# Attention and gated MLP on one core: GpSimd's pieces no longer wait for VectorE's pieces, with a new order of all pieces

## The chip, the cores and the metric

One core of a Trainium2 chip runs the whole kernel in one launch. The metric is the device time of one execution in microseconds (us); lower is better. Engines are named as in the profile: PE (TensorE, with PEld for its weight loads), DVE (VectorE), ACT (ScalarE), POOL (GpSimd), SP (SyncE, which issues nearly all DMAs).

## What is computed

Causal attention with a decay, in 8 batches of 8 heads, 576 positions, head size 64; then an MLP over the 512 joined columns, whose gate is a causal convolution of five taps.

```python
scores = scale * np.matmul(q, k.transpose(0, 1, 3, 2))
cum = np.cumsum(np.log(np.clip(f, 0.0001, 1.0)), axis=-1)
decay = cum[:, :, :, None] - cum[:, :, None, :]
scores = np.where(causal, -1000000000.0, scores + decay)
scores = scores - np.max(scores, axis=-1, keepdims=True)
attn = np.exp(scores)
x = np.matmul(attn / (np.sum(attn, axis=-1, keepdims=True) + 1e-09), v)
...
for k in range(5):
    gate_pre += conv_w[k][None, None, :] * xp[:, k:k + S, :]
out = ((1.0 / (1.0 + np.exp(-gate_pre))) * (x @ w_val)) @ w_out
```

## The kernel before

The 64 heads are worked on as 32 pairs (two heads on 128 partitions); four pairs are one batch. For each pair *i* the stages are:

- **S**: PE forms the scores of three groups of key blocks (L233 is the helper that records every matmul; `banks<-Xr` for q times k, `banks<-st,pk` for the decay). DVE adds the mask and takes the maximum (L423, `negm`), ACT takes the exponential and the row sums (L427, `P`, `zs`).
- **turn**: DVE transposes P in blocks of 32 (L462, `T`). Two copies of T into `U` (L248, class `UC`) run on ACT, POOL or DVE, and four DMAs bring the other quarters (`U<-T`), after the copies into the same tile.
- **reciprocal**: POOL or DVE adds a small number to the nine row sums (L435, `zr`), then DVE forms the reciprocal and transposes it (L439 `zr`, L440 `zt`, two instructions of 9 and 32 columns); DMAs spread `zt` over the partitions (`zd<-zt`, `zb<-zd`).
- **PV**: PE multiplies (`banks<-U,vt`); DVE reads the result out times `zb` into `x` (L519, three instructions).
- **split and gate**: for matmuls of higher precision `x` is split into `xh` (a cast, L248) and `xl` (L528, x minus xh, on POOL or DVE). The gate is a sum of five taps: either a product (L253 on ACT, L255 on POOL or DVE) and a POOL addition (L564, `gate<-gate,tm`), or one DVE instruction (L562). ACT takes the tanh (L569).
- **MLP** of a batch: PE forms the value (`Mv`: `banks<-xh,wall` and `banks<-xl,wall`, in halves of six matmuls for each 128x288 tile, the second half of which uses pairs 2 and 3 of the batch), DVE multiplies with the gate (L595, `h`), which is split into `hh` (a cast) and `hl` (L609, POOL or DVE), PE forms the output (`Mo`: `banks<-wall,hh`, `banks<-wall,hl`), ACT or DVE reads it out (L636, L638), SP stores it.

The decays of pairs 0 to 20 are made at the start (L325 to L345, `st`); those of pairs 21 to 31 in the middle, from `lnf`, which is read back by a DMA (`tm<-lnf`) and then scanned on DVE (L337). The two weights are decoded in the first 80 us (L695 to L711, ACT, DVE and POOL).

The kernel doesn't choose the order of its pieces when it is built: `ORDER` is a compressed table that was planned beforehand. It gives the sequence of all 2354 pieces, the engine of each piece that has a choice, and the PSUM bank of each tile. Each engine does its pieces strictly in that sequence, and the tile framework adds the waits that data need. On top of these the kernel adds one kind of wait by hand: while it goes through the table it remembers the last DVE piece whose class is in `PORT`, and the first instruction of every POOL piece is made to wait for it:

```python
        if e == "POOL" and turn is not None:
            tc.add_manual_dep(done[0], turn.name, wait, reason="shared port")
        elif e == "DVE" and cls in PORT:
            turn = done[-1]
```

`PORT` holds the classes of the weight decode, of the split, of the gate, of the U copies, and `rec`, which is both the nine-column addition (L435) and the reciprocal with its transpose (L439, L440).

Of the kernel before, what the change touches and what calls it, by code (L numbers as in the profile page):

```python
# [41 lines left out]
NS = (21, 11)
ORDER = (
    "c-lQuTTB$`wyvtKzTd0w)%WWAy}SB;@2<Y14~RYp@-QGL5##~UohW*e0o{o(JP5-{1bG;clL&GWKp%v0Cj-Mt6gi0^I}vmeL3bkPB*J(SK~8d{?U{%A>tAbq>s#wv>xV"
    "%EWCD+XUw{X|3t$R(3V^@>Z~_zn?}0af9<T#ba1@XOUVsi_;C*Nkw15OK1fU=eMnD3r0!u&*PzPKBYr$1=J@p}Zk*tAF!i``9&<u8g-CzsQ4s-xrKo4*poQ2jPGyEg?9"
    "sB@ZfHt8aa0IvwK8Bj8I2?vwkO{a0Zh_~(9(V;Ff*0Uva2?!)CxPcsCtQNh!E5kicndyBp;2n!O>!SR0^7)c06&s<;R$$`+)lwLT@;*5P`1bysbAn$Dh%1_db$D@!WUR"
    "9vVt5Vx3Zpr^WX-!N48MD0PjH(Sx**{yD3}H9}rFnQ%V$s(nz^PX{JDwF6td>KSf6ArhcZ@Ll)=>n4<Snv*e@X6XZcEM%x9SP!L)TWr4av{Q_EObZCaULV;*i^jnnMl<"
    "&x+R2-V6%4m<NblMs<3~f^D$;;$+G6HQ;+vpic2I-(<^k3*PP7~=B<ss!hrGwl;#%a6MPN<U{rJbdvX^WHz`ZRr#0`nfQw&@-8b$SoI3OWw;(L3oI^qb@n@(0RW$|p)Y"
    "t&YCS8lpEqBlLY}g|$TQfm)yi)-(DJ{SKK#nxmhf9i_$SS7-;626`WK3-U6292y&AZ?Y~>>uJ5TVcIoX6K$UkP+RDaS<~b-7K?P9g-{VT&Sp?i>L{z9wZ%FI?XkR6kZ~"
    "DeGQQ`?*jj3YF~Nb@2V6bF&QLH0XjfPv>NsnVHN&z|!|XJbPx6o~>}t*r<ez8}5=t6{F0<35IgXYz&mq`HNOhbU+8k|&GeK+NWEnz+kKV*M!MMgc%BW`)sYf}>{1Us1-"  # L50
    "NQM~zQFEfH*n@@=QzixHqsKUhV+zkhOy0A=j?M%k)G4~I3t{CP6ua$v%>+o&7^M9U8sxE&gfutGcsH$?>8F8v+y=)d$e{^KWUIO$hbuMkx}F^xHxZ#)5yEYGc!}nFz+3"
    "smHm+9W`1M<%-bXxcYzmSj`C)BS4qFq9`nX|yR-??ERRkvGHZCvyjtEp(gtasL}TtVYM5QTdN#tW;<ob^`9fY3JIfhhABZQ}B)WipiPz2JbN`bu&EO%g`Blg^f1kfiS|"
    "Uv_>|CE{iao|2W<MkCkYvmSc8ts9|H6F4{GNH8N$_^~OYDAL1krO(a8cxE#vJ=Q#EPu&T96(DMCKW1n0J_I<QSqwzK~v$o-ocK9^{{lT4o=z&VXPa*Dh*fUf{ms*K<FK"
    "JCG^nMG*rT71be~$VIM<zQJR{I%Ws6pLv?uFKXrXaJxiJ+>~U4@r*skTw#uj2ATcbPrMn?OWr#s!tdgCiv~q&%-hUa5zK!mJ>Y%dDfo-hqUe$68p`5ru=m(Q$Q$Nu<UR"
    "X2@&~&{^pW|Jy&`InY>Mh6jUp1KR#YWf5UnFLmYKE6?~v?@#*sZ{vxvtU<Zg-9M4gg7(K$(jM9+s=%SeoG=Px1;5g)%@<YuusJV{iHaAd47ixA(Cr1-bFRtYMRagIqm5"
    "}IsC@)o&|d_W-agk(;lmFPHC{CnJAxxMHo<N(pLvZABnI(`j*S~4PGiX)O2Qkq~>I?nx>J1;rMZ{Tl9Ps;e>CCRR|M}o_qaL@9KtUYO$tXmeA{geAlg2`aPzqsq%ZEiQ"
    "egO3PM0VcT0|B-)}Z{dUmJ6wzGwcsZ~HA^90mfqsu=4S-=_*Q{k>=Wz7%gSMOlQ<@-7oQNXNj^wcm2V}F1lI*e1cVG1K+<+uqpVqm$leJU(p^C<>yqq-;Hh9pur7dPcL"
    "Xy6q4bkPCfgH~WIv%3=rO@Gnq?hGTE!Z9n;4eZrBBg*S(W^ld=8DsYh<&620@2-8@0;k(RH*({6w}Q+ec3c&I<k}nB{xqY55M?A?Orrpj~2yyeJ$Ivm^>>6H71kNe9&5"
    "2{po3GEhzvnuTYCkZ=iY7yc^X2~i;~tQOV@&!|RZw`6?zthhtiC%z^AQGQj}ud0(vRpa8YFeAJt{#6{34yx+4A7l?@2eP*^RNgFqr)*bMNeO9<^t$lAY#5!CJrUm#-Vp"
    "98yHqu*AvvVNRhVi@xTow^T~g6iwW?L=q6|?rX)ox`O2aBbH7B&F28FfK)ABWON%dSjr5;r+spr(s)Qze!`6pSg{EB=`xG29ScWVH20G(H#lfG2F5ucV`mLlkDH3QvOq"  # L60
    "nd5?xN2H;LH<zHs#{huG<?mfN~_sX-_b@iC`uDO6223zXlJy4mo5qyv^`QB{SWDoG>T@>r^1KwSISM*2i2l#Ql8d~NI^}Vrb@G^T^Cw4$23~BK~syat3L{PqPN2P@)pg"
    "O_M&!AxTgK2daE2$AE;RBEwM~=S9%0Jj-E!lv}e)tXt%as`$)bn-;}S&r=^41$J)<YSpCX)Ni(a3MHjRPhG7<LR4c=->xMP`y4xBXI;fk_@YE#510956>QUW&&8o3ivn"
    "4;T`9nUgqhnv>Oa)&dSDeLY`T@<Py2*M?v#HzFTGfbt*xagJ)GTXubw$OBZb64*m>yN*`b+3z-Iner#dnH3iZhC8#f+jIYgg1Mt}7lXEPAcNrtmA)bZPYsMHqXk*wdBN"
    "tD1UDrteVT>WCt(7*d4wGrEt)eIsaMm|kewOnQ;VbX<K_eM-$YL3%>}P%~z}f*r-u*cBa3IgI)2P1se%32atT(yuE{t1s(+Rh(D%VjZSUO_k}GDPr2yY-=v7kLi0%b*3"
    "Sc)ih!fXf?{$3Z4>Gnw9SqxYA?lGo4ZHD!TNo`c`YN{u&lhqNc0rs9LA(G&Pv^6c5Y`=6ZcbNm8awbnTwzu{mV<343FbYyDcA_MLgc)M6UI#`I14Vf_Vtx4OncSSGMJt"
    "kzPpteDr#n5EHzSZ1(YGh~rjo?)BjW{bu0)_BELRNhfen(v#h>DrWZOSN)Jxoyg6BibtMZ`daGJGP7c9|q|r^`A@wdWKG*BWdTcOUi4?J@d3_(X?thFnurz&9zFv_Py0"
    "=>#+`5r}Vg`-EvGjYwEM=bxZnL<%o64x^CUD&gmEQRvoTm*ihSDi^uj%{{*{id1bQOhb>LYWmB((WzKrSx=xGM2AgHN>&okfHbc?iHtgx=tb}gcx?`=<Em>zQFZFNqHM"
    "%-ogN|>zVW>9L8Ez;;2EuUB@VkCjPd5xIpIIlYU51El-r8W0nsM`x0W%lvHFm3+WDpoe3^K!6!$o_oJ#4;f&>1dRFSs6B1}rhpBYVHS%id_;w6EA_?7Q|+`<UgGrP)q1"
    "P8l8<w(LCPp8ca?&E9UynD?zu4G#>T4deDf`>eg&ZZVW>JohiIcKf<v!2mfRBWmohZ5XshmUr0_vq#(u_HEa`%j#aWj45ARb}ec5k_&Y2xaf`>t_jz=>xemHJ8eF0K4p"
    "$N&YEq;_l6<Y-_3tB6OIwrv}@6_ZP~YY+@STD%WbSSHrW=HSFG1;^|p|))z<48uyvSa)*kbi?S$=`tJem5v-Xq5KJ!VBz`EfQIBZtJh`Q%oTK7?h-tofI=&5qIdxmXyY"  # L70
    "!Ke;x$bE&Uh>d!jd#<dvtD)gxEbzI&zx<+#<Yg5TONhO?x=M~yfZeh^|<?pHDf()Z8iEFt&RcrQRBF$&FBlQ*>*jTZF`=6&x~im^Vl=%8T8yRUNqh`)>=o52;SwfdaJ!"
    "2Z`!-!`N`Yj?eVrbmb`P`4(~bdj&0S~<T&BD;2w5&8kc?bj%VIFuNLoeJh#2E9l_t*NcJx_roG2egEzT5z4P7%uhd`TN9+^cX|LSg;plUWJFd7}-LcT5yVp48mg8042k"
    "r&;8UKpA%irg%$M3tB-2ZT#@T_}pI|RNV$6MbOyxZUJZ}(sF4|%t|gZ__>DWlt2bbfZwoFQkm6LPM(?>QD6xSw!_{itulYsZgzeE2~)i(kN-@JVBxlkj8y-yBaI&mEhN"
    "lAq^%U|cZ1^F0mK`Yrw#{yqNQ{f8TMj{3j2cYW(2$iE#r@V4T5pTY}z_I&%HejN5?eQ-qRW%=H?nI5`-C!}?5gnICoew!2V58>6JmQbVrp8xw07~XPd?Y;3&UY~E%|G{"
    "tfEk|R%#pqn9E_5!`;G7R>Jq@9WP)}$mG!i=NeB_*RUU#-RpE@5n7o6+P4d-3|4d+E?F*1!$hx$TAA1knI><E4G9}RUmhn!uJn#fY9G4jeM@W?$jk2LbozwBT2!+}O$o"
    "v+6CKR6!AhDMw>Bkhq{{8zj-vWDMvX2S2Cqme~FBfJp7A}jbzBpmtZycB8nbw_xv&(5l_B{Ca%kH5ho7ZG_J8Nr();}NOrb(9xlxlV)+{H(|yIOf`pGNOX8FFX+E1*|b"
    "Nwjb?}$in(?EZpbo^zB4FF);RB%<a01uSC#5RqR--C)N=|qFBHhSc`Z9mwo4bKlpC@w6QyZTfTd~yS|@&d$`Bb5<3^`jP=DfBBemc^)yiJvWHv4rvjNkefS{K6kbgo51"
    "bC14V({L4nzWxSUNTpNW10&^S+a=7lF+HBX%b~6CaAz#V&?t<1gaogx#fxeu%tE2_yRGFabv|gg-_4!(HJ9*Si3cfD+@e&G_@!nP5-2CNUC|CGLi66T9)f_(B{{5Q)ce"
    "dSWXcPJ9g92&~8U11s^XfqUWZz<-BJiJ!xR;oIR`iMHVL@Xf%-6qXnb?58y8NV+j$P1mIv>8f-p3I^u`%pjOH2YJDVu~_s;V2o(W`l9w|U6h}$4oZVH(b2@KXjSxl6bm"
    "kePX^t=j$kC%7<?K2_h?&sDBTsk9}8vP5zDc+u~t`Wb}arWwi@-Mn-dM`W9f}>Ita%<#1>-*v2^-<_(<?v;!47vpG*wLdlLhRx2dBpT6`qk8Ei@Sq@m0%u}2V@jx?6R;"  # L80
    "%NLva4_1J?o2mkkjxLksbEcJB8|j<h`vc%G7V8Qy`7e2ZU#q!^h|B0IrAVmAH0@08!crX5G%wQ0pz0bAEV>Zd+FQJd(j2rF=5TMXFR!dd@8%1-6W31E%6Vj`w3ruG4V9"
    "<DZQL{m{?D2Cm6Yd^m33z2#Lwy_t~G*N8&K?G`N{Sb4%HwES}lU?u50uk?eh9HGMa;lbFdYrypisr5Dqu;u~3h?p*w1up{G*&t+c(H-fX#e~a%Yda^C?%kk>ujpTgxO7"
    "?T`Wb$URFZ(Rpn4HLhAuu_bEao5O*-0r;lfRnT$)3;2le_uhOeD9GN0Pc^M{YlBC3-WH#BydJGnT2%zsjs;vUy8#FTa-WjN`<`JVx~ANArz&Z;}<dlibX2<!ACl?pp3c"
    "@ItmZKc0^#OT?KZk*vzi=8qHalDyPZQkrT@HW20%FZ49&PJK*DLobpY$+={E{uEK4JCR#R4(3bA&g2hCsPH;-j%dm~Nrs88e0M%lSje9xE)yAIKS>lelURyg_&d>>i{%"
    "G$i<zT^-drTLo7v9nXQ1qz+*s~Lijh@j`2}qVOtls5h2fmOpeXnXCkpk2)<RRk9wJgm7R&Y!bGe1wOwN&IrrgD1ajMvsYAeLEc(y9Fl<Oldrikpna;5C?Y*(SD&{3$(u"
    "H^a(|C@W6>q-q3wsZSAa-NZ=6{k|yiw}yt;>DsUKUzSG|5ZTq|0v89779y+>SCx!6rUG97H$+j7wU@Ie08d!*qi#TaJKlU_#pMPcrpbQHw#+@ZP8j>FAf!NrW#YNsrgh"
    "_aiO?T94$^1w~HT(ywc~QyCf}zO4X&2)MRQo1(jH(bg8X$vV@iFrN+|HQfujAsk78uf&mBs0RSKaq^~FR^@ITmKn1?}$>qqQeHi)n9irhf{?L2)0bdd13g$2ZmTlmxhf"
    ">b?#tW92;jb3>H9{)iDPJv8ndOibsNla<CzTn<m5jrB<iF75az43y1Iv}+O65ZzQ0|agMo`Kapu$Qi>p8@eD+(!PcA(4$mbngXQaSINHn<!C%E)gS;9vZQvBOSDWkrWw"
    "fR#$*ik3fhQY&|IMJe>xw8`aqK)Fk>oJ%d&`cpSl{!_|51LX>oiege3{VnU;4xzFiD09N)`9Xi}g;Hjtl$DbztcNj51x+d6DdjG|%?GT!338<mxH5B~q6(;JqL!xvmv>"
    "C9%m%9b$rTk~ISy2`ft7txDvF@L{6M)+xUz9lWy+)q-=A*{s(692VyIjR{Oe8r`ELFnvP;#~"  # L90
)
# [702 lines left out]
```

## Time and profile before

| what | value |
|---|---|
| device time, median of 3 runs | 459.16 us (458.07 to 460.58) |
| device time of the profiled execution | 463.08 us |
| its span, first to last instruction | 461.0 us |
| PE busy | 423.9 us, 92% of the span |
| DVE busy | 382.9 us, 83% |
| ACT busy | 332.3 us, 72% |
| POOL busy | 309.4 us, 67% |

The span is what the trace covers; 2.08 us of the profiled execution lie around it. The profiled execution is 0.85% longer than the median of the runs. Rows of the trace give start and length in us from the start of the span; a number in square brackets is how long the engine sat idle before that row, and the name behind `<-` is what ended that wait.

### The profile page before, as it was taken

The numbers are of one execution on the slowest core, as the hardware profiler recorded it, in microseconds if no ns is written. First come the engines' busy times: TensorE is split into PE (matmuls) and PEld (weight loads), VectorE is DVE, ScalarE is ACT, GpSimd is POOL, SyncE is SP. The second block draws the span as 40 slices with busy tenths as digits, with TensorE's granted clock in tenths as the row PEclk, the third lists the DMA queues.
The fourth block names the chain that finished last, engine by engine and source line by source line (L and its number), as shares of the span: only waits on it lengthen the run. The fifth ranks groups of instructions, "written<-read, shape, count | busy, mean of one in ns | idle before, by whom it ended". The sixth has DMA issues, their size and how long they took to land.

```text
span 461.0 us, 16758 instructions
## 1 busy us (share of the span) xinstructions
PE 423.9 (92%) x6640; PEld 359.9 (78%) x6640; DVE 382.9 (83%) x1034; ACT 332.3 (72%) x836; POOL 309.4 (67%) x310
## 2 busy tenths in 40 slices
...
GB/s 287 283 129 249 213 190 241 198 118 261 186 248 163 209 171 197 274 232 206 211 199 100 136 239 215 219 181 204 132 246 192 188 206 173 223 118 129 23 70 114
DMA packets 74847, 87.23 MB, mean 189 GB/s; under 512 B 48145, under 2 KB 48145, under 8 KB 74769
## 3 DMA queue, kind: packets, MB, share of 16 engines
...
q8 instruction: 52, 0.85, 0.9%
q10 hardware_dynamic: 144, 0.29, 0.2%
q14 instruction: 27, 0.21, 0.2%
...
## 4 chain that ended last, share of the span: by engine, by line
PE 47%; POOL 13%; DVE 13%; DMA 12%; issue 6%; SPq 5%; ACT 3%; POOLq 0%; DVEq 0%; ACTq 0%
PE banks L233 47%; POOL gate L564 6%; SPq L260 5%; DMA zb<-zd 4%; DVE banks L423 4%; DVE T L462 3%; DMA U<-T 2%; DMA vt<-in_v_dram 2%; POOL xl L528 2%; POOL U L248 2%; ACT P L427 2%; DMA sh<-in_w_val_dram 1%; POOL tm L255 1%; DMA zd<-zt 1%; DMA tm<-lnf 1%
## 5 line engine op out<-in xcount | busy, mean ns | idle before, releaser
L427 ACT ACTIVATE P<-banks,negm 128x384 f32<-128x384 f32 (+8 forms) x288 | 149.6, 528 | 46.4 <-DVE negm L423 36.4
L564 POOL TENSOR_TENSOR gate<-gate,tm 128x576 f32<-128x576 f32 x82 | 117.5, 1434 | 42.6 <-DVE tm L255 14.7
L423 DVE CUSTOM_DVE_ANT_0 banks<-banks,mk 128x512 f32<-128x512 f32 (+8 forms) x288 | 135.1, 504 | 9.6 <-PE banks L233 6.7
L462 DVE STREAM_TRANSPOSE T<-P 128x1088 f32<-128x1088 f32 (+2 forms) x96 | 110.9, 1166 | 6.6 <-DMA U<-T 3.5
L233 PE MATMUL banks<-xh,wall 128*128 128x288 f32 x512 | 108.8, 298 | 1.7 <-ACT P L427 0.9
L233 PE MATMUL banks<-Xr 64*64 64x288 f32 (+8 forms) x1280 | 103.2, 410 | 2.5 <-DMA Xr<-in_x_dram 2.5
L233 PEld LDWEIGHTS banks<-U,vt 64*64 64x64 f32 x3456 | 92.3, 136 | 14.1 <-issue 10.1
L233 PE MATMUL banks<-U,vt 64*64 64x128 f32 (+1 forms) x3456 | 93.2, 257 | 9.6 <-ACT sh L695 4.0
L233 PE MATMUL banks<-wall,hh 128*128 128x512 f32 x288 | 91.6, 399 | 0.0
L233 PEld LDWEIGHTS banks<-xh,wall 128*128 128x128 f32 x512 | 84.3, 189 | 6.0 <-ACT P L427 1.6
L233 PE MATMUL banks<-xl,wall 128*128 128x288 f32 x256 | 76.0, 297 | 4.1 <-POOL xl L528 3.9
L233 PEld LDWEIGHTS banks<-Xr 64*64 64x64 f32 x1280 | 65.0, 134 | 15.8 <-issue 5.1
L233 PEld LDWEIGHTS banks<-wall,hh 128*128 128x128 f32 x288 | 52.3, 189 | 13.2 <-DVE negm L423 1.3
L233 PE MATMUL banks<-st,pk 64*64 64x288 bf16 (+8 forms) x640 | 48.6, 297 | 11.3 <-ACT P L427 6.5
L233 PE MATMUL banks<-wall,hl 128*128 128x512 f32 x144 | 56.9, 395 | 2.3 <-POOL hl L609 2.3
L427 ACT ACTIVATION_READ_ACCUMULATOR P<-banks,negm 128x1 f32 x288 | 58.4, 203 | 0.0
L248 ACT COPY U<-T 128x1440 f32<-128x1440 f32 x37 | 51.3, 1396 | 5.9 <-PE banks L233 5.2
L233 PEld LDWEIGHTS banks<-xl,wall 128*128 128x128 f32 x256 | 48.4, 189 | 5.4 <-POOL xl L528 4.1
L233 PEld LDWEIGHTS <-pk 64*64 64x64 bf16 x640 | 26.5, 107 | 29.6 <-issue 24.9
L609 POOL TENSOR_TENSOR hl<-h,hh 128x576 fp32r<-128x576 f32 (+2 forms) x39 | 40.9, 1068 | 11.5 <-DVE gate L562 4.4
L528 POOL TENSOR_TENSOR xl<-x,xh 128x576 fp32r<-128x576 f32 x24 | 34.7, 1446 | 15.9 <-DVE zt L440 10.4
L519 DVE TENSOR_TENSOR x<-banks,zb 128x256 f32<-128x256 f32 (+1 forms) x96 | 30.8, 345 | 11.5 <-PE banks L233 5.5
(103 smaller groups left out, 495.8 us busy)
## 6 DMA issues: line engine op xcount, KB each, us to landing
U<-T SPq DMA_DIRECT2D x128, 180.0 KB
...
```

The lines of the kernel that those rows point to most:

```text
L233: nc.tensor.matmul(out, lhsT=lhsT, rhs=rhs, start=start, stop=stop)
L248: (eng.copy if eng is nc.scalar else eng.tensor_copy)(out=out, in_=in_)
L255: eng.tensor_scalar(out=out, in0=in_, scalar1=col, scalar2=0.0, op0=ALU.mult, op1=ALU.add)
L260: lambda e: (nc.sync if e == "SP" else nc.scalar).dma_start(out=out, in_=in_), reads, writes, dma=span)
L423: nc.vector.tensor_tensor_reduce(out=sl, in0=sl, in1=mk[:, S - ext:], op0=ALU.add, op1=ALU.min, scale=-0.125, scalar=3.0e38, accum_out=neg ...
L427: nc.scalar.activation(out=dst, in_=bank(key)[:, a0:a0 + ext], func=AF.Exp, bias=negm[r][:, col], scale=-1.0, accum_out=zs[r][:, col])
L462: nc.vector.transpose(out=bass.AP(Tt.tensor, Tt.offset + 32 * FB[js[0]], [pitch, (32, nk), (CW, 2), (1, 32)]), in_=Pt[u])
L519: nc.vector.tensor_tensor(out=bass.AP(to.tensor, to.offset, [to.ap[0], *dims, (1, D)]), in0=bank(keys[y])[:, D * first:D * last].rearrange ...
L528: any_("xl", {"POOL": 1.4, "DVE": 0.67}, p, lambda eng: eng.tensor_tensor(out=xl[s], in0=xv, in1=xh[s][:, :].bitcast(F32), op=ALU.subtract ...
L564: eng.tensor_tensor(out=gt, in0=gt, in1=to, op=ALU.add)
L609: eng.tensor_tensor(out=hl[jj][:, y:y + x1 - x0], in0=h2[jj % 2][:, x0:x1], in1=hh[jj][:, y:y + x1 - x0].bitcast(F32), op=ALU.subtract)
```

## The change

`PORT` becomes empty, so no POOL piece waits for a DVE piece because of the port; waits that data need stay. The piece of the reciprocal and its transpose gets a class of its own, `recT`, which nothing in the kernel reads. The table `ORDER` is another one (47 lines, of which the first is shown): it has the same 2354 pieces in another sequence, with other engines for 244 of them.

```diff
-PORT = {"wv", "wo", "rec", "xh", "xl", "diag", "conv", "cvm", "cva", "hh", "hl", "UC"}
+PORT = set()
 NS = (21, 11)
 ORDER = (
-    "c-lQuTTB$`wyvtKzTd0w)%WWAy}SB;@2<Y14~RYp@-QGL5##~UohW*e0o{o(JP5-{1bG;clL&GWKp%v0Cj-Mt6gi0^I}vmeL3bkPB*J(SK~8d{?U{%A>tAbq>s#wv>xV"
+    "c-mD`c}QIOmae<hzVB7H_FMa2b!*?NZtW%y)Z~w7JJ8xbh{gxT_CYimXe)UTZ3onLAQ}f+<3M73pmqkL?LccBh{ge99Ec_j(PSW+JV@+3h{iuADeVVyFPGmv=X~co-#N"
...
-        dve("rec", 0.36, p, turn, [("zr", r)], [("zr", r), ("zt", r)])
+        dve("recT", 0.36, p, turn, [("zr", r)], [("zr", r), ("zt", r)])
```

**Pair 15.** Names carry buffer numbers here: `xl3` and `x321` are those of pair 15, `zr1` and `zt1` those of pair 17. On POOL before, between the row sums of pair 17 and the gate of pair 15:

```order
L435 TENSOR_SCALAR zr1_94<-zs1_92 128x9 [waits Activation_49]
L528 TENSOR_TENSOR xl2_109<-x320_99,xh2_103 128x576 [waits PE_49]
L248 COPY U1_85<-T1_83 128x1440 [waits DMAHW3_49,DMAHW7_49,DVE_49,PE_49]
L528 TENSOR_TENSOR xl3_110<-x321_100,xh3_104 128x576 [waits DVE_49,Activation_49]
L255 TENSOR_SCALAR gate_113<-x321_100,cw_65 128x576
L564 TENSOR_TENSOR gate_113<-gate_113,tm_78 128x576 [waits DVE_49,Activation_49]
```

On POOL now, at the same place:

```order
L435 TENSOR_SCALAR zr1_94<-zs1_92 128x9 [waits Activation_49]
L248 COPY U1_85<-T1_83 128x1440 [waits DMAHW2_49,DMAHW4_49,DVE_49,PE_49]
L248 COPY U1_85<-T1_83 128x1440 [waits DMAHW3_49,DMAHW0_49]
L255 TENSOR_SCALAR gate_113<-x321_100,cw_65 128x576
L564 TENSOR_TENSOR gate_113<-gate_113,tm_78 128x576 [waits Activation_49,Pool_49]
L255 TENSOR_SCALAR tm_78<-x321_100,cw_65 128x576 [waits Pool_49]
```

The piece `xl3` has left POOL. On DVE before, the second half of the decays of pairs 21 to 31 (its scan L337 stands four rows further up) with the reciprocal of pair 17 (L439, L440) behind it:

```order
L423 ISA banks_122,negm0_89<-banks_122,mk_73 128x256
L423 ISA negm0_89 128x1
L423 ISA banks_122,negm0_89<-banks_122,mk_73 128x448
L423 ISA negm0_89 128x1
L248 CAST st1_71<-tm_78 128x576
L423 ISA banks_122,negm0_89<-banks_122,mk_73 128x320
L423 ISA negm0_89 128x1
L345 SCALAR_TENSOR_TENSOR tm_78<-st1_71,sel_72,tm_78 128x576
L423 ISA banks_122,negm0_89<-banks_122,mk_73 128x64
L423 ISA negm0_89 128x1
L439 RECIPROCAL zr1_94<-zr1_94 128x9
L440 STREAM_TRANSPOSE zt1_96<-zr1_94 128x32
```

On DVE now, from the readout of pair 15:

```order
L519 TENSOR_TENSOR x321_100<-banks_122,zb1_98 128x2x2x64
L519 TENSOR_TENSOR x321_100<-banks_122,zb1_98 128x64
L519 TENSOR_TENSOR x321_100<-banks_122,zb1_98 128x2x2x64
L423 ISA banks_122,negm0_89<-banks_122,mk_73 128x448
L423 ISA negm0_89 128x1
L439 RECIPROCAL zr1_94<-zr1_94 128x9
L440 STREAM_TRANSPOSE zt1_96<-zr1_94 128x32
L423 ISA banks_122,negm0_89<-banks_122,mk_73 128x64
L423 ISA negm0_89 128x1
L528 TENSOR_TENSOR xl3_110<-x321_100,xh3_104 128x576
L337 SCALAR_TENSOR_TENSOR tm_78<-one_123,tm_78 128x576
L339 TENSOR_SCALAR ref1_125<-tm_78 128x1
```

The reciprocal of pair 17 and `xl3` now stand on DVE in front of the scan L337.

**The value matmuls of pair 15.** On PE before, from the end of the score group that follows PV of pair 15 (`hh`, `hl` belong to the output of the batch before):

```order
L233 MATMUL banks_122<-Xr0_75 64x64 x2
L233 MATMUL banks_122<-wall_119,hh_1262 128x512 x2
L233 MATMUL banks_122<-wall_119,hl_1439 128x512
L233 MATMUL banks_122<-wall_119,hh_1262 128x512 x2
L233 MATMUL banks_122<-wall_119,hl_1439 128x512
L233 MATMUL banks_122<-xh0_101,wall_119 128x288
L233 MATMUL banks_122<-xl0_107,wall_119 128x288
L233 MATMUL banks_122<-xh0_101,wall_119 128x288
L233 MATMUL banks_122<-xh1_102,wall_119 128x288
```

On PE now, from the end of the second score group that follows PV of pair 15:

```order
L233 MATMUL banks_122<-Xr0_75 64x128 x2
L233 MATMUL banks_122<-Xr0_75 64x384 x2
L233 MATMUL banks_122<-Xr0_75 64x256 x2
L233 MATMUL banks_122<-xh0_101,wall_119 128x288
L233 MATMUL banks_122<-xl0_107,wall_119 128x288
L233 MATMUL banks_122<-xh0_101,wall_119 128x288
L233 MATMUL banks_122<-xh1_102,wall_119 128x288
L233 MATMUL banks_122<-xl1_108,wall_119 128x288
L233 MATMUL banks_122<-xh1_102,wall_119 128x288
```

Before, one score group, one half of an output tile and four value halves of pairs 12 and 13 (`xh0`, `xl0`, `xh1`, `xl1`) and one triple of pair 14 stood between PV of pair 15 and the first use of `xl3`; now two score groups, two such value halves and one triple of pair 14 stand there.

**The first U copies.** On POOL before, from the row sums of pair 0 to the second copy into `U0`:

```order
L435 TENSOR_SCALAR zr0_93<-zs0_91 128x9 [waits Activation_49]
L362 MEMSET x321_100 128x4
L536 TENSOR_TENSOR tm_78<-ident_64,cw_65 128x640 [waits DMAHW5_49]
L248 COPY U0_84<-T0_82 128x1440 [waits DVE_49]
L363 MEMSET zr1_94 128x32
L707 TENSOR_TENSOR wall_119<-ot_118,sh_116 128x512 [waits DMAHW7_49,Activation_49]
L248 COPY U0_84<-T0_82 128x1440
```

On POOL now, from the second weight sum:

```order
L701 TENSOR_TENSOR sl_117<-sl_117 128x512 [waits Activation_49]
L435 TENSOR_SCALAR zr0_93<-zs0_91 128x9 [waits Activation_49,Pool_49]
L707 TENSOR_TENSOR wall_119<-sl_117 128x512 [waits DMAHW7_49]
L248 COPY U0_84<-T0_82 128x1440 [waits DVE_49]
L362 MEMSET x321_100 128x4
L248 COPY U0_84<-T0_82 128x1440
L707 TENSOR_TENSOR wall_119<-ot_118,sh_116 128x512 [waits DMAHW6_49,Activation_49]
```

The weight product from `ot` that stood between the two copies into `U0` now stands behind both, and the one from `sl`, which stood behind them, stands ahead of both.

## Rows read from the trace of the kernel before

**Rows 1.** Page, part 1: busy us (share) and instructions of each engine.

```profile
PE 423.9 (92%) x6640; PEld 359.9 (78%) x6640; DVE 382.9 (83%) x1034; ACT 332.3 (72%) x836; POOL 309.4 (67%) x310
```

**Rows 2.** Windows: length, busy PE, PEld, DVE, ACT, POOL; PEclk, DMA share, GB/s.

```profile
0.00:37.00 37.00, 20.63 (x226) 15.08 (x230) 30.31 (x87) 25.97 (x65) 22.41 (x51) 0.88 0.70 234
37.00:457.00 420.00, 402.93 (x6418) 344.84 (x6416) 352.62 (x948) 305.74 (x772) 286.98 (x260) 0.99 0.69 186
457.00:461.00 4.00, 0.38 (x2) 0.00 (x0) 0.00 (x0) 0.60 (x1) 0.00 (x0) 1.00 0.35 131
```

**Rows 3.** Tile zt: ns min/median/max; then who waited for it (us, times).

```profile
L440 DVE STREAM_TRANSPOSE zt<-zr x32: 210/211/215, 26.5 to 411.9; 128x32 f32<-128x32 f32 x32
...
  POOL xl L528: 10.4, 5
```

**Rows 4.** Timeline by engine, around the xl of pair 15.

```profile
227.13 0.67 ACT L248 CAST xh<-x 128x576 fp32r<-128x576 f32 x1
...
228.23 1.36 DVE L337 TENSOR_TENSOR_SCAN tm<-one,tm 128x576 f32<-128x576 f32 x1 [1.36 <-DMA tm<-lnf]
...
232.90 0.21 DVE L440 STREAM_TRANSPOSE zt<-zr 128x32 f32<-128x32 f32 x1
...
233.26 1.45 POOL L528 TENSOR_TENSOR xl<-x,xh 128x576 fp32r<-128x576 f32 x1 [5.60 <-DVE zt L440]
...
234.77 0.40 PE L233 MATMUL banks<-xl,wall 128*128 128x288 f32 x1 [3.89 <-POOL xl L528]
```

**Rows 5.** Windows inside the value matmuls, before and after that wait.

```profile
227.00:230.00 3.00, 3.00 (x24) 2.99 (x23) 1.74 (x4) 0.98 (x4) 0.66 (x1) 1.00 0.85 224
...
236.00:239.00 3.00, 3.00 (x10) 2.41 (x9) 0.46 (x1) 1.47 (x5) 0.00 (x0) 0.51 1.00 291
```

**Rows 6.** Timeline of POOL and PE, around the hl that PE waits for.

```profile
254.80 0.74 POOL L255 TENSOR_SCALAR gate<-x,cw 128x576 f32<-128x576 f32 x1 [3.79 <-DVE zt L440]
...
261.62 4.10 POOL L609 TENSOR_TENSOR hl<-h,hh 128x64 fp32r<-128x64 f32 x4
...
264.53 0.50 PE L233 MATMUL banks<-wall,hl 128*128 128x512 f32 x1 [2.29 <-POOL hl L609]
```

**Rows 7.** Timeline of POOL, SP's queue and PE, around the first PV.

```profile
26.82 1.38 POOL L248 COPY U<-T 128x1440 f32<-128x1440 f32 x1 [2.54 <-DVE zt L440]
...
30.86 1.18 SPq L260 DMA_DIRECT2D U<-T  x2
...
36.79 1.54 PE L233 MATMUL banks<-U,vt 64*64 64x128 f32 x24 [4.03 <-ACT sh L695]
```

**Rows 8.** DVE instructions of three lines: ns min/median/max, first and last start.

```profile
L528 DVE TENSOR_TENSOR xl<-x,xh x8: 717/1104/1676, 67.4 to 428.0; 128x576 fp32r<-128x576 f32 x8
...
L562 DVE SCALAR_TENSOR_TENSOR gate<-x,cw,gate x38: 777/816/1703, 75.9 to 437.1; 128x576 f32<-128x576 f32 x38
...
L255 DVE TENSOR_SCALAR tm<-x,cw x4: 515/516/1411, 126.7 to 434.6; 128x576 f32<-128x576 f32 x4
```

**Rows 9.** Timeline of DVE and POOL: two DVE pieces that meet a POOL piece.

```profile
10.25 1.95 DVE L345 SCALAR_TENSOR_TENSOR gate<-st,sel,gate 128x576 f32<-128x576 bf16 x1
...
284.44 2.90 POOL L564 TENSOR_TENSOR gate<-gate,tm 128x576 f32<-128x576 f32 x2
...
286.24 1.41 DVE L255 TENSOR_SCALAR tm<-x,cw 128x576 f32<-128x576 f32 x1
...
439.21 1.30 DVE L609 TENSOR_TENSOR hl<-h,hh 128x64 fp32r<-128x64 f32 x2 [1.34 <-ACT hh L248]
```

**Rows 10.** Timeline of PE, the output half ahead of the value matmuls of pair 15.

```profile
225.52 0.72 PE L233 MATMUL banks<-wall,hh 128*128 128x512 f32 x2
...
227.01 0.29 PE L233 MATMUL banks<-xh,wall 128*128 128x288 f32 x1
```

**Rows 11.** Timeline of DVE, from the readout of pair 31 to its xl.

```profile
425.71 0.89 DVE L519 TENSOR_TENSOR x<-banks,zb 128x256 f32<-128x256 f32 x3 [1.78 <-PE banks L233]
...
427.96 0.75 DVE L528 TENSOR_TENSOR xl<-x,xh 128x576 fp32r<-128x576 f32 x1
```

92 lines of the change are left out of this document (46 added, 46 removed).

## The prediction

> **What bounds the kernel now.** I read the shares of the engines first, then the windows by stage, then who waited for whom, and last the timeline around the long waits of PE. PE is busy 92% of the span, DVE 83%, POOL 67% [rows 1]: PE sets the time, and what a change can give is PE's idle time, plus matmuls that ran at the lower clock. Of the 461.0 us, 37.1 are idle on PE: 37.00 - 20.63 = 16.4 in the first 37 us, 420.00 - 402.93 = 17.1 in the 420 us after them, 3.6 behind the last matmuls [rows 2]. The change touches no matmul, so the 423.9 us of PE work stay, and the last 3.6 us (readout and store of the last tile) stay too.
>
> **What is removed.** A wait of POOL for the DVE pieces that stand ahead of it in the table. Its clearest form is a wait for the reciprocal's little transpose (`zt`). That instruction took 210 to 215 ns in all 32 cases although POOL is busy two thirds of the time [rows 1, 3], so nothing shows that it ever met a POOL piece at a port, and yet POOL's xl pieces alone sat idle 10.4 us behind it [rows 3]. Idle time of POOL costs nothing by itself; three of these waits reach PE.
>
> *First, the xl of pair 15.* Its input was ready when the cast ended, 227.13 + 0.67 = 227.80, and POOL fell idle at 233.26 - 5.60 = 227.66. It began 5.60 us later, because it had to wait for the `zt` of pair 17, which ended at 233.11; that one sat on DVE behind a scan that waited for the DMA of the second decays. PE waited 3.89 us for this xl [rows 4]. Started at 227.80, with its own 1.45 us, it would have ended at 229.25, and PE wanted it at 234.77 - 3.89 = 230.88: the whole 3.89 us go. Behind the gap the granted clock was 0.51 from 236 to 239 us, the lower of its two levels, where it had been 1.00 before [rows 5]; PE was busy for all those 3.00 us, and work at 0.51 would take about half as long at 1.00, so another 1.5 us go. What is late next there: nothing on POOL. In the new order `xl3` is on DVE, and both it and the reciprocal stand ahead of the scan, so the late DMA no longer holds anything that pair 15 needs.
>
> *Second, an hl piece.* POOL sat idle 3.79 us for another `zt` at 254.80 and then worked without a break up to the hl pieces at 261.62, for which PE waited 2.29 us [rows 6]. Without the 3.79 us the hl pieces come earlier by more than PE's wait: 2.29 us go.
>
> *Third, the first PV.* The first copy into U began 2.54 us late on POOL, again for `zt`; a weight product and the second copy followed, the last two DMAs of U were issued from 30.86 on, and PE stood still for 4.03 us until 36.79 [rows 7]. The profile names ACT as what ended that wait; since those DMAs had still to land, I hold a transfer to be the cause. The ends of the gain are nothing, if something else held PE, and 2.54 us. In the new order nothing but a small fill stands between the two copies, but on DVE more maxima stand ahead of the third transpose of pair 0, and on SP the DMA of `zt` stands ahead of the U DMAs. I take 1.5 us, nearer the upper end, since a weight product has also gone from between the two copies.
>
> **What is added or moved.** *Work between engines.* Counted in both orders, the one-instruction taps on DVE (L562) go from 38 to 43, products on DVE (L255) from 7 to 12, xl on DVE from 8 to 9, and hl instructions on DVE from 9 to 14; three U copies leave DVE. With the medians of the rows, 5 x 0.82 + 5 x 0.52 + 0.72 = 7.4 us [rows 8], with the hl about 3 us more and the copies about as much less: some 7 us more on DVE, which is idle for 461 - 383 = 78 us. I cost it at nothing; where that cover is thin, as in the first 37 us, DVE's idle time is 37.00 - 30.31 = 6.7 us [rows 2], and the shift there is one weight piece. POOL has less to do than before.
>
> *Collisions.* A DVE piece that starts while POOL works can be held until POOL has ended: the product at 286.24 took 1.41 us instead of 0.52 and ended 0.31 us after the POOL addition beside it, at 287.65 against 284.44 + 2.90 = 287.34; xl took up to 1.68 instead of 0.72 us [rows 8, 9]. This happened in spite of the waits to 17 DVE pieces, the first at 10.25 and the last at 439.21 [rows 9], by 0.7 us each on average, 12 us in all, since the old waits kept POOL from starting ahead of DVE, not DVE from starting inside a POOL piece. Without them POOL also gets ahead where DVE runs late. The Trainium skill (SBUF — State Buffer, section "Who interferes with whom") speaks against the change here: it calls the shared pair of ports an exclusive lock, held for a whole instruction by whichever side issues first, and counts copies, casts, tensor_scalar and instructions with two SBUF inputs among those that take it on DVE. By that rule a free POOL hands DVE up to a whole POOL piece of delay each time; the trace agrees in the 0.31 us between the two ends. From the rows alone: about 110 DVE pieces of the new order are of the kinds that can be held. Below, no more than the 17 are held, and the cost is nothing; above, POOL's share of 67% of them are, some 74, which is 57 more than now and 57 x 0.7 = 40 us more on DVE. I take ten more, 7 us on DVE, of which a fifth reaches PE as DVE is idle 17% of the time: 1.5 us.
>
> *Shorter leads.* In the new order PE comes to the first value matmul of pair 15 sooner after its PV: two value halves and an output half have become one more score group. A value half takes 0.75 us (24 matmuls in 3.00 us, six to a half) [rows 5], the output half took 227.01 - 225.52 = 1.49 us [rows 10]; the score group in its place I take as equally long, an estimate from that row. So the lead loses 2 x 0.75 = 1.5 us. Before, it was 1.49 us, four halves and a triple of pair 14 of 0.375 us, 4.9 us, and one score group ahead of them; now it is 3.4 us and the same score group, about 1.5: 4.9 us in all. The least that the chain needs, from the first readout to the end of xl, is 428.71 - 425.71 = 3.00 us with DVE doing the xl [rows 11], so it fits with some 1.9 us to spare. In the new order a maximum and a reciprocal also stand between readout and xl on DVE; two held DVE pieces use the rest up. The other seven batches have leads of this kind too, most of them shorter than before. Nothing is lost below; above, one held piece of 0.7 us too many in half of them costs 3 us. I take 1.
>
> **The sum**, on the profiled execution's own time: 461.0 - 3.89 - 1.5 - 2.29 - 1.5 + 1.5 + 1.0 = 454.3 us of span, and with the 2.08 us around it 456.4 us. The profiled execution, 463.08 us, is 0.85% above the median of the runs; 456.4 x 459.16 / 463.08 = 452.5. New waits that a whole new order brings can't be read in the old trace; I round up to **453.0 us**, 1.3% below the median.
>
> **The rivals.**
> *The waits weren't what held PE.* Of the 17.1 us in the middle, some 11 are many small waits that have nothing to do with POOL, and a new sequence has small waits of its own. If the two large gaps are replaced by others of their size (one late DMA of U before a PV is enough), the change does not do what it says and only the startup moves: 459.16 - 1 = about 458. For it: the xl gap needed a late DMA as well as the wait. Against it: both gaps name POOL as what PE waited for, and both times POOL was idle for `zt` just before.
> *VectorE becomes the bound: slower.* POOL runs ahead wherever DVE is late, DVE pieces are held, DVE gets later still. The place is every stage in which DVE has little room, the first 60 us above all. It decides from about 45 held pieces on: 28 more than now, at 0.7 us, are 20 us on DVE, a quarter of its idle time; if half of that reaches PE, 10 us eat up the 9.2 us gained. With 60 held pieces, 43 x 0.7 / 2 = 15 us are lost and the time is 459.16 + 15 - 9.2 = 465. For it: DVE at 83% and the 17 pieces held already. Against it: what a wait cost POOL was up to 5.60 us, what a collision costs DVE about 0.7.
> *More is gained.* The small waits on ACT and on U also lie behind pieces that POOL did late; if 7 more of the 17.1 us go, 446.
>
> **How the numbers follow.** Chances: the forecast 0.52, no gain 0.17, VectorE as the bound 0.19, more gained 0.12. The likeliest case alone spans 449 to 457 by the bounds of its terms; with the others the range that should hold the time 8 times in 10 goes from 446 to 464. About 0.5% (2.3 us) is what a measurement can tell from no change here. Faster than 456.9: the forecast but for its upper edge and the case of more, 0.61; within 0.5%: 0.19; slower than 461.5: 0.20.
>
> **What would show it.** Right: no POOL row that waits for `zt`; no gap of PE over 2 us behind an xl or hl of POOL; POOL's idle time no longer led by DVE's names; held DVE pieces between 20 and 35 in number; PE idle 6 to 10 us less in the middle. Wrong: L562, L528 and L255 on DVE with medians well above 0.82, 0.72 and 0.52 us; DVE busy over 395 us; PE waiting for DVE readouts or maxima where it waited for POOL before; or a gap in front of a PV with a low granted clock behind it, which a new order may bring whatever POOL waits for.

## The result, and the profile after

The changed kernel takes 443.57 us (median of 4 runs, 442.11 to 445.24), the kernel before on the same chip 458.7 us (458.07 to 460.58): a ratio of 0.9665, 95% interval 0.9618 to 0.9712, so 15 us or 3.35% faster. The prediction said 453.0 us and 446 to 464: the direction was right, the size was not. Medians and spans of runs here take in all runs of a kernel; the ratios leave disturbed runs out.

The profiled execution took 443.04 us. Page, part 1 (busy us, share, instructions), and the granted clock of PE in 40 slices, in tenths of the full 2.4 GHz:

```profile
PE 419.3 (95%) x6640; PEld 357.3 (81%) x6640; DVE 381.8 (87%) x1045; ACT 336.0 (76%) x834; POOL 290.6 (66%) x296
...
PEclk9989999999999999999999999999999999999999
```

Windows of the changed kernel, with the columns of [rows 2]:

```profile
0.00:37.00 37.00, 25.39 (x327) 18.08 (x331) 31.19 (x93) 28.18 (x76) 24.30 (x52) 0.95 0.74 248
37.00:437.70 400.70, 393.88 (x6325) 339.18 (x6316) 350.57 (x953) 307.18 (x758) 266.27 (x244) 1.00 0.72 194
437.70:441.30 3.60, 0.00 (x0) 0.00 (x0) 0.00 (x0) 0.60 (x1) 0.00 (x0) 0.87 0.39 146
```

Against [rows 1, 2], PE's idle time fell from 16.4 to 37.00 - 25.39 = 11.6 us in the first 37 us and from 17.1 to 400.70 - 393.88 = 6.8 us in the middle; the tail stayed at 3.6. PE's busy time fell by 4.6 us too; the granted clock is higher in both stretches, 0.95 where it was 0.88 and 1.00 where it was 0.99.

Who PE waited for, and who POOL waited for, in the changed kernel (us in total, times, longest us), the first rows of each; then the tile `zt` with who waited for it:

```profile
PE banks L233 <- ACT P L427: 9.4, 12, 2.1
PE banks L233 <- DVE x L519: 2.0, 2, 1.8
PE banks L233 <- DMA U<-T: 1.7, 2, 1.4
PE banks L352 <- POOL ebias L294: 1.4, 1, 1.4
...
POOL gate L564 <- DVE tm L255: 20.4, 4, 7.5
POOL gate L564 <- DVE gate L562: 13.9, 7, 4.5
...
L440 DVE STREAM_TRANSPOSE zt<-zr x32: 211/211/215, 24.6 to 399.1; 128x32 f32<-128x32 f32 x32
...
  PEld banks L233: 0.4, 1
```

The gaps behind xl and hl [rows 4, 6] are gone: POOL stands in PE's list with one wait, 1.4 us for a constant at the very start. POOL no longer waits for `zt` (10.4 us for xl alone in [rows 3]). It still waits for DVE, 34.3 us in these two rows, but for data: the taps that L564 adds.

The 32 transposes take as long as before although POOL now works beside most of them: 28 overlap a POOL piece and 21 of these lie wholly inside one, where it was 13 and 10 in the kernel before. One of the 21:

```profile
342.65 1.41 POOL L564 TENSOR_TENSOR gate<-gate,tm 128x576 f32<-128x576 f32 x1
...
343.06 0.21 DVE L440 STREAM_TRANSPOSE zt<-zr 128x32 f32<-128x32 f32 x1
```

DVE's three lines (ns min/median/max), to set beside [rows 8]:

```profile
L528 DVE TENSOR_TENSOR xl<-x,xh x9: 745/752/760, 125.3 to 410.5; 128x576 fp32r<-128x576 f32 x9
...
L562 DVE SCALAR_TENSOR_TENSOR gate<-x,cw,gate x43: 776/812/1376, 73.0 to 418.3; 128x576 f32<-128x576 f32 x43
...
L255 DVE TENSOR_SCALAR tm<-x,cw x7: 510/515/517, 156.9 to 407.5; 128x576 f32<-128x576 f32 x7
```

No xl on DVE is held any more (longest 0.76 us, 1.68 before). Counted as in the prediction (a piece over 0.1 us longer than its kind takes when it is free), 13 DVE pieces are held, by 7.5 us in all; before it was 17 and 12.

### The profile page after: what moved, and what is told of

Read it like the earlier page. It is cut to its first block, busy times and chain, and to the rows that moved or that the text cites. A ratio compares the mean times of both kernels' runs of the same rounds, so it can differ in the third digit from the quotient of the medians.

```text
span 441.3 us, 16739 instructions
## 1 busy us (share of the span) xinstructions
PE 419.3 (95%) x6640; PEld 357.3 (81%) x6640; DVE 381.8 (87%) x1045; ACT 336.0 (76%) x834; POOL 290.6 (66%) x296
## 4 chain that ended last, share of the span: by engine, by line
PE 58%; DMA 3%; DVE 1%; SPq 0%; issue 0%; ACT 0%; DVEq 0%; ACTq 0%
PE banks L233 58%; DMA U<-T 1%; DMA zb<-zd 1%; DMA out_dram<-ot 1%; DMA zd<-zt 1%; SPq L260 0%; DVE gate L255 0%; DVE xl L528 0%; DVE h L595 0%; DVE x L519 0%; ACT ot L636 0%; DVE tm L255 0%; DVE zt L440 0%; DVE zr L439 0%; DVEq L519 0%
## 5 line engine op out<-in xcount | busy, mean ns | idle before, releaser
L427 ACT ACTIVATE P<-banks,negm 128x512 f32<-128x512 f32 (+8 forms) x288 | 149.5, 528 | 41.8 <-DVE negm L423 31.1
L564 POOL TENSOR_TENSOR gate<-gate,tm 128x576 f32<-128x576 f32 x77 | 110.7, 1439 | 58.5 <-DVE tm L255 20.4
L462 DVE STREAM_TRANSPOSE T<-P 128x1024 f32<-128x1024 f32 (+2 forms) x96 | 110.8, 1165 | 10.8 <-DMA U<-T 6.2
L233 PE MATMUL banks<-Xr 64*64 64x288 f32 (+8 forms) x1280 | 104.9, 415 | 1.2 <-DMA Xr<-in_x_dram 0.8
L233 PEld LDWEIGHTS banks<-U,vt 64*64 64x64 f32 x3456 | 89.8, 133 | 8.5 <-issue 2.8
L248 ACT COPY U<-T 128x1440 f32<-128x1440 f32 x44 | 61.2, 1395 | 7.2 <-issue 4.4
L233 PE MATMUL banks<-st,pk 64*64 64x256 bf16 (+8 forms) x640 | 47.9, 291 | 11.8 <-ACT P L427 8.4
L233 PEld LDWEIGHTS <-pk 64*64 64x64 bf16 x640 | 27.9, 106 | 27.8 <-issue 22.7
L609 POOL TENSOR_TENSOR hl<-h,hh 128x576 fp32r<-128x576 f32 (+2 forms) x34 | 36.2, 1080 | 7.1 <-ACT tm L253 3.4
L423 DVE DVE_READ_ACCUMULATOR2_ANT negm<- 128x1 f32 x288 | 39.8, 138 | 0.0
```

The costliest lines, as they stand in the source:

```text
L233: nc.tensor.matmul(out, lhsT=lhsT, rhs=rhs, start=start, stop=stop)
L248: (eng.copy if eng is nc.scalar else eng.tensor_copy)(out=out, in_=in_)
L423: nc.vector.tensor_tensor_reduce(out=sl, in0=sl, in1=mk[:, S - ext:], op0=ALU.add, op1=ALU.min, scale=-0.125, scalar=3.0e38, accum_out=neg ...
L427: nc.scalar.activation(out=dst, in_=bank(key)[:, a0:a0 + ext], func=AF.Exp, bias=negm[r][:, col], scale=-1.0, accum_out=zs[r][:, col])
L462: nc.vector.transpose(out=bass.AP(Tt.tensor, Tt.offset + 32 * FB[js[0]], [pitch, (32, nk), (CW, 2), (1, 32)]), in_=Pt[u])
L564: eng.tensor_tensor(out=gt, in0=gt, in1=to, op=ALU.add)
```

## The experiments

All of them change `PORT` or the class of the reciprocal's piece, the only piece that makes `zt`. The order of pieces is always that of before ("old") or that of the change ("new"). The waits are no data waits, so any of them may be left out.

### Waits and order, each alone

**old_no_waits**: the old order, all waits dropped.

```diff
-PORT = {"wv", "wo", "rec", "xh", "xl", "diag", "conv", "cvm", "cva", "hh", "hl", "UC"}
+PORT = set()
```

> Old order, waits dropped (PORT empty). Theory 1 (the waits held PE, and the new order only uses the freedom): the gap of 3.89 us for the xl of pair 15, the half clock behind it and the gap of 2.29 us for the hl go, 1.5 us at the first PV too: 459 - 8 to 9 = about 450 us, more than half of the 15 us gained. Theory 2 (the new order itself gained it; the waits were harmless in it): within 2 us of before, 457 to 459. Theory 3 (collisions: without waits and without an order made for it DVE is held more often): slower, 461 or more, with over 25 held DVE pieces.

Measured: 442.45 us (440.98 to 445.1), ratio 0.9657 (0.9615 to 0.9699). The old order without its waits is as fast as the change, and some 8 us faster than the theory behind the prediction had it (450).

**old_not_zt**: the old order, `PORT` as before, only the waits behind the reciprocal dropped.

```diff
-        dve("rec", 0.36, p, turn, [("zr", r)], [("zr", r), ("zt", r)])
+        dve("recT", 0.36, p, turn, [("zr", r)], [("zr", r), ("zt", r)])
```

> Old order, only the waits behind the reciprocal's transpose dropped (class recT). Theory 1: the three waits that the prediction priced are all waits for zt, so this gains as much as old_no_waits, about 450 us. If the chain of waits only moves to the DVE piece ahead of the zt (POOL then waits for that one), it gains less than half of what old_no_waits gains. Theory 2: within 2 us of before.

Measured: 442.49 us (440.0 to 443.86), ratio 0.9633 (0.9591 to 0.9675). One word does all of it: the other waits of the old order cost nothing that shows. Page, part 1, of old_not_zt and then of old_no_waits:

```profile
PE 419.6 (95%) x6640; PEld 357.8 (81%) x6640; DVE 377.0 (85%) x1034; ACT 331.9 (75%) x836; POOL 307.7 (70%) x310
```

```profile
PE 418.8 (95%) x6640; PEld 356.6 (81%) x6640; DVE 385.5 (88%) x1034; ACT 332.1 (75%) x836; POOL 312.9 (71%) x310
```

Dropping the other waits as well costs DVE 8.5 us (23 pieces held against 10), and the time doesn't move: DVE has the room.

**new_all_waits**: the new order, `PORT` as before and the reciprocal's class `rec` again, so all waits are back. **new_waits_not_zt**: the same, but the class stays `recT`.

> New order with every wait put back, that on the reciprocal's transpose too (its class is rec again). Theory 1: the waits cost in the new order what they cost in the old one, 6 us or more: 450 or above. Theory 2: 444 to 446. Theory 3: the waits guard DVE, so it is faster than the change, below 443.

> New order with the waits put back except that behind the reciprocal's transpose (class recT stays unread). If the cost of the waits is that of the false one alone (zt met no POOL piece in any row of before), this is within 1.5 us of the change, 443 to 445, whatever new_all_waits shows. If all kinds of waits cost, it lies midway between the change and new_all_waits.

Measured: 447.87 us (446.32 to 449.23), ratio 0.9768 (0.973 to 0.9806), with all waits; 440.77 us (437.85 to 442.05), ratio 0.9605 (0.9561 to 0.9648), without those for `zt`. So the new order gains 458.31 - 447.87 = 10.4 us where the false waits stand, and nothing where they don't (442.45 against 443.57; the ratios, 0.9657 and 0.9665, compare them on their own chips). With all waits the new order still leaves POOL idle for `zt` for 26.6 us, against 32.9 in the kernel before, but no wait of PE names POOL there except the one at the very start: the pieces that PE needs have moved out of the way. The two halves of the change are two cures of one illness, and their gains don't add: 15.8 and 10.4 make 15. In the new order too the waits for `zt` cost 447.87 - 440.77 = 7.1 us.

**zt_only**: the old order, and the reverse of old_not_zt: POOL waits for sums and reciprocals and for nothing else.

```diff
-PORT = {"wv", "wo", "rec", "xh", "xl", "diag", "conv", "cvm", "cva", "hh", "hl", "UC"}
+PORT = {"rec"}
```

> Old order; PORT holds rec alone: POOL waits for the sums and reciprocals, all its other waits for the port are dropped. Theory 1 (the reciprocal's waits are the cost, the others cost nothing): as slow as before, 456 to 460 us. Rival (all kinds of waits share the cost, and old_not_zt gained because the chain of them was broken): midway, 449 to 452.

Measured: 462.69 us (460.86 to 464.3), ratio 1.0115 (1.004 to 1.0191): about 1% slower than before, where the same time was expected. Beside the false waits the others seem to be worth something: DVE's part of the page and its xl pieces here:

```profile
PE 423.5 (92%) x6640; PEld 359.1 (78%) x6640; DVE 390.1 (85%) x1034; ACT 332.6 (72%) x836; POOL 313.7 (68%) x310
...
L528 DVE TENSOR_TENSOR xl<-x,xh 128x576 fp32r<-128x576 f32 x8 | 10.4, 1305 | 0.7 <-ACT xh L248 0.6
```

28 DVE pieces are held, by 19.0 us; xl takes 1.305 us on average, where the change has 0.75. That these held pieces are what costs the 1% is likely but not shown: above, 13 more of them cost nothing.

### Which of the 32 waits

**zt_first6** and **zt_rest**: the old order; the reciprocals of pairs 0 to 5, or of pairs 6 to 31, make nothing wait. **zt_pair17**: that of pair 17 alone.

```diff
-        dve("rec", 0.36, p, turn,
+        dve("recT" if i < 6 else "rec", 0.36, p, turn,
```

```diff
-        dve("rec", 0.36, p, turn,
+        dve("rec" if i < 6 else "recT", 0.36, p, turn,
```

```diff
-        dve("rec", 0.36, p, turn,
+        dve("recT" if i == 17 else "rec", 0.36, p, turn,
```

> Old order; only the reciprocals of pairs 0 to 5 (before some 92 us) make no POOL piece wait. Read beside each other, matmul by matmul, old_not_zt leads before by 4.9 us at 92 us and by 18.9 us at the end. Theory 1 (each wait costs where it stands, the costs add): this run keeps the 4.9 us: 458.3 - 4.9 = 453.4 us. Rival (one late chain: time lost early is what makes the later waits long): most of the 16 us, below 448. Rival (slack eats the early gain): 457 or more.

> Old order; the reciprocals of pairs 6 to 31 make no POOL piece wait, those of pairs 0 to 5 still do. Theory 1: it gains the other 14.0 us of the lead: 458.3 - 14.0 = 444.3 us, and with zt_first6 the two gains add up to the 16 to 19 us of old_not_zt. Rival (one late chain that begins in the startup): under 6 us gained, above 452.

> Old order; only the reciprocal of pair 17 makes no POOL piece wait: the first term of the prediction by itself. If the prediction's working holds, the gap of 3.89 us behind xl of pair 15 is gone, the clock behind it stays at 1.00, and 5.4 us are gained: 453 us. If POOL's next wait takes its place (for a DVE piece ahead of the reciprocal, or the hl 30 us later grows), 2 us or less is gained, 456 or more.

Measured: zt_first6 455.21 us (451.41 to 460.23), ratio 0.9903 (0.9854 to 0.9952); zt_rest 447.84 us (447.41 to 449.66), 0.9799 (0.9731 to 0.9868); zt_pair17 451.35 us (450.42 to 453.61), 0.9883 (0.9799 to 0.9968). On 458.4 us that is 4.4, 9.2 and 5.4 us. The first two make 13.6 us, against 16.8 by the ratio of old_not_zt: within their intervals the costs add, and there is no sign of a chain from the startup through the kernel. The 9.2 us are less than the 14.0 expected of zt_rest. Pair 17 alone gives what the prediction had for it, 3.89 + 1.5, with a wide interval of 1.5 to 9.2 us.

Since these kernels have one order, the same matmul can be looked up in two traces. Starts in zt_first6 and in old_not_zt, which differ by the waits of pairs 6 to 31:

| matmul of PE | zt_first6 | old_not_zt | lead |
|---|---|---|---|
| a score matmul (q times k) | 157.60 | 158.93 | -1.3 |
| first value matmul that needs xl of pair 15 | 225.98 | 223.30 | 2.7 |
| an output matmul (`hh`) right after these value matmuls | 229.56 | 225.29 | 4.3 |
| the hl matmul of [rows 6] | 255.75 | 248.94 | 6.8 |

The lead grows by 1.6 us behind the xl gap, where zt_first6 runs at a granted clock of 0.55 from 226 to 229 us, and by 2.5 us at the hl: the prediction's 1.5 and 2.29. Behind the hl it grows by 1.7 us more, to 8.5 us, since in zt_first6 the clock falls there too while PE is busy without a break:

```profile
257.00:260.00 3.00, 3.00 (x16) 1.98 (x18) 2.27 (x4) 0.46 (x2) 3.00 (x4) 0.50 0.84 199
```

In before and before_again it stays at 1.00 behind the hl gap, so there the gap costs its own length alone. The first value matmul in zt_first6 carries the whole gap still:

```profile
225.98 0.41 PE L233 MATMUL banks<-xl,wall 128*128 128x288 f32 x1 [3.63 <-POOL xl L528]
```

**three_waits** and **other_29_waits**: the three waits that the prediction priced, and all the others.

```diff
-        dve("rec", 0.36, p, turn,
+        dve("recT" if i in (0, 17, 18) else "rec", 0.36, p, turn,
```

```diff
-        dve("rec", 0.36, p, turn,
+        dve("rec" if i in (0, 17, 18) else "recT", 0.36, p, turn,
```

> Old order; only the reciprocals of pairs 0, 17 and 18 make no POOL piece wait: these are the three waits that the prediction priced, all three at once and nothing else. By the prediction's terms 1.5 + 3.89 + 1.5 + 2.29 = 9.2 us are gained: 458.4 - 9.2 = 449.2 us. By the rows read beside each other (pair 17: 4.5 and 0.9; the hl 2.5 and 0.8; the first PV 2.9) it is 11.6 us: 446.8. If the other 29 waits hold PE as well, they take these gains' place: 452 or more.

> The complement: the reciprocals of all pairs but 0, 17 and 18 make no POOL piece wait; the three priced waits stay. If the prediction was right that three of these waits reach PE, this gains nothing: 457 to 459. If old_not_zt's gain of 15.9 us is a sum of many small waits beside the three, this gains the difference, 4 to 7 us: 451.4 to 454.4. If the three exist only because POOL comes late to them, their gaps shrink here, and it gains 8 or more: 450 or less.

Measured: three_waits 447.98 us (445.62 to 455.51), ratio 0.9781 (0.9728 to 0.9833), 10.0 us of 457.85; other_29_waits 453.44 us (451.59 to 455.11), ratio 0.9904 (0.9869 to 0.9939), 4.4 us. The sum of the three terms is right, 10.0 us (7.6 to 12.5) for 9.2, and the others are not nothing. Of the three, the first PV seems worth more than the 1.5 us taken. In the old order it starts at 34.77 to 36.79 us in the six executions in which POOL waits for the `zt` of pair 0, and at 32.26 to 32.73 us in the four in which it doesn't: 3.5 us earlier on average. The lead lasts: the first value matmul starts at 71.97 to 75.39 us in the six, at 70.12 us in three_waits. The first PV there:

```profile
32.46 1.75 PE L233 MATMUL banks<-U,vt 64*64 64x128 f32 x61 [0.92 <-ACT P L427]
```

What POOL still idled for `zt`, in three_waits and then in other_29_waits:

```profile
POOL tm L255 <- DVE zt L440: 6.3, 3, 3.3
POOL xl L528 <- DVE zt L440: 5.1, 4, 2.2
POOL gate L564 <- DVE zt L440: 5.0, 2, 3.8
POOL gate L255 <- DVE zt L440: 2.7, 1, 2.7
POOL U L248 <- DVE zt L440: 1.2, 1, 1.2
```

```profile
POOL xl L528 <- DVE zt L440: 5.7, 1, 5.7
POOL gate L255 <- DVE zt L440: 3.8, 1, 3.8
POOL U L248 <- DVE zt L440: 2.5, 1, 2.5
```

The 12.0 us of idle POOL behind three waits cost 10.0 us of kernel, the 20.3 us behind the others 4.4. How long POOL idles tells little; who stands behind it tells the price.

### The kernel before once more

**before_again**: no edit, one execution.

> The kernel before once more, for its rows: the execution that the prediction was read from took 463.08 us, 4.7 us above the median of all runs of before. If its gaps at 67.0, 87.98 and 285.73 us and the stretches at half the clock before 42 us belong to that one execution, they are smaller here and the time is 457 to 460 us, while the gaps behind xl (3.9 us) and hl (2.3 us) and at the first PV (4.0 us) stand. If they belong to the kernel, all of them stand here too.

Measured: 459.92 us. The gaps at 67.0, 87.98 and 285.73 us don't come back, that at the first PV is 1.9 instead of 4.0 us; those behind xl and hl stand:

```profile
231.67 0.40 PE L233 MATMUL banks<-xl,wall 128*128 128x288 f32 x1 [3.48 <-POOL xl L528]
...
261.43 0.50 PE L233 MATMUL banks<-wall,hl 128*128 128x512 f32 x1 [2.30 <-POOL hl L609]
```

Windows of before_again, as [rows 2]:

```profile
0.00:37.00 37.00, 23.25 (x254) 17.11 (x258) 30.60 (x89) 26.43 (x67) 23.27 (x51) 0.83 0.71 237
37.00:454.20 417.20, 401.50 (x6393) 344.52 (x6386) 351.97 (x948) 305.03 (x770) 287.08 (x260) 0.99 0.69 187
```

PE idles 13.8 and 15.7 us here, and 16.4 and 17.1 us in [rows 2]: about 4 us that the prediction was read from belong to that one execution. Of the 20.0 us between the two profiled executions, 463.08 and 443.04, some 15 are the change and the rest is chance.

The trace also shows what a wait among the 29 does. Rows of POOL, DVE and PE in before_again, around the reciprocal of pair 10:

```profile
138.22 0.21 DVE L440 STREAM_TRANSPOSE zt<-zr 128x32 f32<-128x32 f32 x1
...
138.61 2.92 POOL L564 TENSOR_TENSOR gate<-gate,tm 128x576 f32<-128x576 f32 x2 [3.81 <-DVE zt L440]
...
141.56 0.82 DVE L562 SCALAR_TENSOR_TENSOR gate<-x,cw,gate 128x576 f32<-128x576 f32 x1 [2.82 <-POOL gate L564]
...
145.01 1.34 DVE L595 SCALAR_TENSOR_TENSOR h<-gate,banks 128x288 f32<-128x288 f32 x3
...
145.48 0.27 PE L233 MATMUL banks<-st,pk 64*64 64x192 bf16 x4 [1.01 <-DVE h L595]
```

POOL waits 3.81 us for `zt`; DVE's next tap waits 2.82 us for POOL's sums; the multiplications L595 come late, and PE waits 1.01 us for a bank that they free. PE's row names DVE, two steps from the cause. The same pieces in other_29_waits, where the reciprocal of pair 10 holds nothing:

```profile
136.33 1.44 POOL L564 TENSOR_TENSOR gate<-gate,tm 128x576 f32<-128x576 f32 x1 [0.49 <-ACT tm L253]
...
138.17 0.81 DVE L562 SCALAR_TENSOR_TENSOR gate<-x,cw,gate 128x576 f32<-128x576 f32 x1
...
142.24 1.18 DVE L595 SCALAR_TENSOR_TENSOR h<-gate,banks 128x288 f32<-128x288 f32 x3 [0.22 <-PE banks L233]
```

POOL's sum is done before the transpose of pair 10 begins, the tap follows without a wait, and now L595 waits for PE. A second one in before_again begins with a POOL wait of 2.94 us for another `zt`, behind which POOL works without a break, and goes through ACT:

```profile
331.25 0.75 POOL L255 TENSOR_SCALAR gate<-x,cw 128x576 f32<-128x576 f32 x1 [2.94 <-DVE zt L440]
...
351.39 0.68 ACT L569 ACTIVATE gate<-gate 128x576 f32<-128x576 f32 x1 [2.15 <-POOL gate L564]
...
352.58 1.18 PE L233 MATMUL banks<-U,vt 64*64 64x128 f32 x30 [1.26 <-ACT P L427]
```

ACT stands 2.15 us at a tanh for a late gate, the exponentials behind it are late, and PE waits 1.26 us for `P`. In other_29_waits both gaps are gone.

### What collisions cost in the new order

**new_waits_not_zt_2** and **after_2**: the new order with its other waits, and the changed kernel, side by side on one chip.

> The new order with the waits for VectorE's pieces other than the reciprocal put back, a second time, beside the changed kernel on one chip: 440.8 against 443.6 us before. If held VectorE pieces cost PE time in the new order (the prediction's 1.5 us for collisions), this stays 1.5 to 3 us under after_2: 440 to 442. If the difference was chance and collisions cost nothing, both are within 1 us of each other, 442 to 444.

> The changed kernel once more, unchanged, as the partner of new_waits_not_zt_2: 443 to 444.5 us by its first runs, with 10 to 16 held VectorE pieces against 5; if the collisions cost nothing, equal to its partner within 1 us.

Measured: 439.54 us (437.35 to 440.84, 6 runs), ratio 0.9621 (0.958 to 0.9661), against 441.52 us (439.19 to 443.02, 6 runs), ratio 0.9652 (0.9609 to 0.9695). The means of the six runs, 439.52 and 441.31, differ by 1.8 us; from their scatter the 95% interval is 0.1 to 3.5. In the first pair of runs it was 440.77 against 443.57. 4 DVE pieces are held in the one, by 1.8 us, 13 in the other, by 7.0. Held pieces probably cost some 2 us there, and the new order with waits for all but `zt` is the fastest version seen, by about 0.4%; the ratios' intervals overlap, so it isn't settled.

## Why the prediction was right in its direction and wrong in its size

The forecast was 459.16 - 453.0 = 6.2 us of gain; 15 came. By its own steps:

1. *The cause* was right. Waits for `zt` held POOL for nothing: dropping these alone gives 0.9633, and the transpose took 211 to 215 ns in all 32 cases of the change as well, 28 of them beside a POOL piece. The Trainium skill (SBUF — State Buffer, section "Who interferes with whom") says why such a wait guards nothing: a DVE instruction with at most one SBUF input, outside the modes that use both ports, does not contend with GpSimd. The rows of `zt` agree.
2. *The three priced waits* were right in sum: 9.2 us predicted, 10.0 measured (7.6 to 12.5). Pair 17 by itself is 5.4 (1.5 to 9.2) for 5.4, and the hl 2.5 for 2.29. The first PV was sized too low as far as the traces show: 1.5 us, with 2.54 as its upper end, where it starts 3.5 us earlier; no run drops the wait of pair 0 alone.
3. *The step that failed* is "three of these waits reach PE", with its companion that "some 11 are many small waits that have nothing to do with POOL". The other 29 waits, costed at nothing, are worth 4.4 us (2.8 to 6.0), about half of the 9 us by which the gain was missed; the rest is the 0.8 us by which the three waits gave more, the 2.5 us of losses of step 4 that have no net effect, and 0.5 us of rounding, within intervals of some 2 us. I had followed PE's gaps one step back, to DVE, ACT or a transfer, and stopped where the name was not POOL. Followed further, the chain reaches POOL, behind `zt`: the rows of 1.01 and 1.26 us show it. This is the rival "more is gained", to which I gave 0.12 and 446 us; its mechanism was the right one, its gain still too small.
4. *The losses* of 1.5 us for collisions and 1.0 us for shorter leads. I expected 27 held pieces and the change has 13. The old order without waits has 23, near the forecast; it is the new order that has fewer, and why was not followed. In the old order 13 more held pieces cost no time (442.45 against 442.49); in the new one the price is probably about 2 us, close to the 1.5, with fewer pieces. For the shorter leads nothing shows: the two orders without waits stand at 0.9657 and 0.9665, which is inside the scatter. So a loss was there in part, and something of the same size may stand against it: with all waits but those for `zt`, the new order is 1.7 us faster than the old (440.77 against 442.49), also inside the scatter.
5. *The order* was not weighed by itself. It takes 10.4 us off where the false waits stand and nothing without them; the prediction read the moved `xl3` and reciprocal as part of the gain, and dropping the wait alone would have done.
6. *"The 423.9 us of PE work stay"* did not hold in the trace: 419.3. 1.6 us of it are the clock behind the xl gap, which the sum did price. The rest does not look like chance alone: before_again has 424.8 us and after_2 420.5, though PE was at a low clock in the startup of both (last section). Part of it seems to belong to the first wait: over the first 42 us the granted clock was 0.80 to 0.88 in the seven executions in which POOL waits for the `zt` of pair 0, and 0.88 to 0.96 in the eight in which it doesn't. The sum had no clock term for that wait. Where the rest of the 4.6 us lies stays open.

Of what was to be seen: no POOL row waits for `zt`, right; no gap over 2 us behind POOL's xl or hl, right; PE idle 10.3 us less in the middle instead of 6 to 10, of which some 1.4 are the old execution's own (before_again idles 417.20 - 401.50 = 15.7 us there, not 17.1); DVE's medians not above the old free times (0.81, 0.75 and 0.52 us) and DVE busy under 395 us, right; POOL's idle time no longer led by DVE's names, wrong, it still is, for data; 20 to 35 held pieces, wrong. The rivals "the waits weren't what held PE" and "VectorE becomes the bound" both fell: old_not_zt and old_no_waits.

What stays open: which of the 29 waits make up the 4.4 us beyond the two followed above, whether the remaining waits pay in the new order, and what made zt_only slower.
